# Transposing the normalized activations of three of four chunks by DMA in place of TensorE

## The chip, the core and the metric

The kernel runs on one core of a Trainium2 chip. The metric is the device time of one execution in microseconds (us), as the median of three runs; beside it stands one profiled execution, whose trace tells where each engine was busy. The engines are named as the profile names them: PE is TensorE (PEld its weight loads), DVE is VectorE, ACT is ScalarE, POOL is GpSimd, SP is SyncE, which here issues DMAs alone (SPq in the trace).

## The reference

The input `x` has 2048 rows of 512 bf16 values. Each row is normalized, and the result goes into two branches whose product is added to `x`:

```python
xn = _layernorm(x, axis=-1)
s = _A_ref(xn, A_wqkv, A_wo)                       # attention
g = _silu(_B_ref(xn, B_w_gate, B_w_up, B_w_down))  # gated MLP
return x + s * g
# A: q, k, v = xn @ wqkv; 32 heads of 16; each row attends to itself and
#    to the rows 2, 4, ..., 14 before it; softmax; output @ wo
# B: h = gelu(xn @ w_gate) * (xn @ w_up), 1792 wide; output h @ w_down
```

[...] the normalized rows (rows on partitions) have to be transposed (features on partitions) before the projections `wqkv`, `w_gate` and `w_up` can use them.

## The kernel before

The 2048 rows are 16 tiles of 128 rows, in 4 chunks of 512 (chunk j holds tiles 4j to 4j+3). The order of all instructions on each engine is written out by hand; engines meet through semaphores.

For each tile, `moments` (L169) takes mean and variance on VectorE and the reciprocal root on GpSimd, `normalize` (L179) writes the normalized tile `xn` (128x512) on VectorE, from a pool of four buffers, and `transpose` (L186) makes four 128x128 transposes on TensorE into one PSUM tile `tr`, which ScalarE copies (L194) to a quarter of `xnT`, the transposed chunk (128 x 4 x 512). `xnT` has two buffers; `xnT` of chunk 2 takes the place of chunk 0's.

For each chunk there are three stages, and the program's order is glu 0, qkv 1, down 0, glu 1, qkv 2, down 1, and so on, after a beginning that makes qkv 0:

- `qkv` j: 12 groups of four matmuls with `xnT` of chunk j: four each for q, k and v. ScalarE evicts each. The v part is stored through SyncE's queue to a DRAM tensor `vT` (L235), and `load_v` (L243) loads it back in another layout as `v_arr`, in four DMAs.
- `glu` j: 14 steps of `g_ps` and `u_ps` (four matmuls each), with Gelu and a copy on ScalarE (`ge`, `u`, three buffers each) and their product `h` on VectorE. PSUM has five buffers that all these results share.
- `down` j: for each tile 14 matmuls with `wd_sb` and four with `wo_sb`, then the product, the residual and the store of the output (L387).

The attention of chunk j is spread over these stages with the table `side`: `at(key, fn, ...)` (L395) places a function ahead of a step, and `run` calls it. The products q*k (`pk`), logits and exponentials come first; `av_product` (L311) makes `pv` from the exponentials and `v_arr` on VectorE, eight per chunk; `av_sums` sums four of them at a time on TensorE into `o_ps` (L325). For chunk 0, `pv` 0 and 1 stand at steps 12 and 13 of glu 0, `pv` 2 to 7 in qkv 1, and the first `o_ps` ahead of qkv 1's fourth group (step 3). For later chunks `pv` i stands at step 2+i of glu j and `o_ps` at step 7.

The same table places the layer norm: normalize of chunk 1 in qkv 0, its transposes at glu 0's first four steps; normalize of chunk 2 at steps 8 to 11 of glu 0, its transposes in qkv 1; normalize and transposes of chunk 3 in qkv 2.

SyncE issues nearly all DMAs, in program order: the loads of `x`, `wqkv`, `w_gate` and `w_up` at the start; the vT stores of chunk 0; its four `v_arr` loads; then `load_late_weights` (L102): `wd_sb`, 1792 KB, and four parts of `wo_sb`, 128 KB each. In the rest of the program come, for each chunk, four vT stores (in qkv), and in the down stage before it is used four `v_arr` loads, one ahead of each output store. An instruction of SyncE that waits holds up all that stand behind it. The completion semaphores of DMAs are eight, taken in turn, so that a DMA may have to wait until the one eight before it has landed.

Of the kernel before, what the change touches and what calls it, by code (L numbers as in the profile page):

```python
# [10 lines left out]
BF16 = mybir.dt.bfloat16  # L11
F32 = mybir.dt.float32

P = 128
# [7 lines left out]
TQ = 512  # L22
# [6 lines left out]
def kernel(  # L29
# [13 lines left out]
    nc = tc.nc  # L43
    B, S, D = A_x.shape
    DF = B_w_gate.shape[1]
    NT, NC, NF, NJ = S // P, D // P, DF // P, S // TQ
    TPQ = TQ // P
# [5 lines left out]
    def pool(name, bufs, **kw):  # L53
        return ctx.enter_context(tc.tile_pool(name=name, bufs=bufs, **kw))
# [9 lines left out]
    xtp = pool("xtp", 2)  # L64
# [38 lines left out]
    def load_late_weights():  # L103
        nc.sync.dma_start(out=wd_sb[:], in_=B_w_down.rearrange("(k p) n -> p k n", p=P))
        for g in range(NC):
            nc.sync.dma_start(
                out=wo_sb[:, g, :],
                in_=bass.AP(
                    tensor=A_wo.tensor, offset=g * 4 * D, ap=[[D, 4], [DH * D, H], [1, D]]
                ),  # L110
            )
# [7 lines left out]
        out=vT.rearrange("(k p) n -> p k n", p=P)[:, :, 0:PAD],  # L119
        in_=warm[:, 0 : NC * PAD].rearrange("p (k n) -> p k n", k=NC),  # L120
# [38 lines left out]
    xnT = {}  # L159
# [17 lines left out]
    xns = {}  # L177
# [22 lines left out]
    def warm_up(n, cols):  # L200

        ps = mm.tile([P, TQ], F32, name="warm_ps", tag="mm")
        for _ in range(n):
            nc.tensor.matmul(
                ps[:, 0:cols], lhsT=warm[:, 0:P], rhs=warm[:, 0:cols], start=True, stop=True
            )

    def project(ps, w, lo, j, i0=0, n=TQ):
        for dk in range(NC):
            nc.tensor.matmul(  # L210
                ps[:],
                lhsT=w[:, dk, lo : lo + P],
                rhs=xnT[j][:, dk, i0 : i0 + n],
                start=(dk == 0),
                stop=(dk == NC - 1),
            )
# [3 lines left out]
    def qkv(j, fo, i0=0, n=TQ):  # L220
        which, c = divmod(fo, NC)
        if fo == 0 and i0 == 0:
            st[j]["q"] = qp.tile([P, NC, TQ], BF16, name="q_sb")
        ps = mm.tile([P, n], F32, name="qkv_ps", tag="mm")
        project(ps, wqkv_sb, fo * P, j, i0, n)
        if which == 0:
            nc.scalar.activation(out=st[j]["q"][:, c, i0 : i0 + n], in_=ps[:], func=AF.Copy)  # L227
        elif which == 1:
            lo = PAD + j * TQ + i0
            nc.scalar.activation(out=k_sb[:, c, lo : lo + n], in_=ps[:], func=AF.Copy)  # L230
        else:
            vst = sm4.tile([P, TQ], BF16, name="vst")
            nc.scalar.activation(out=vst[:], in_=ps[:], func=AF.Copy)  # L233
            lo = PAD + j * TQ
            nc.sync.dma_start(out=vT[c * P : (c + 1) * P, lo : lo + TQ], in_=vst[:])  # L235

    def load_v(j, wls=range(WL)):

        if wls[0] == 0:
            st[j]["va"] = vap.tile([P, DH, VW], BF16, name="v_arr")  # L240
        va = st[j]["va"]
        for wl in wls:
            nc.sync.dma_start(  # L243
                out=va[H * wl : H * (wl + 1), :, :],
                in_=bass.AP(
                    tensor=vT.tensor,
                    offset=PAD + j * TQ - WL * DIL - DIL * wl,
                    ap=[[SV * DH, H], [SV, DH], [1, VW]],
                ),
            )  # L250
# [93 lines left out]
    def glu(j, fc):  # L344
        g_ps = mm.tile([P, TQ], F32, name="g_ps", tag="mm")
        project(g_ps, wg_sb, fc * P, j)
        u_ps = mm.tile([P, TQ], F32, name="u_ps", tag="mm")
        project(u_ps, wu_sb, fc * P, j)
        ge = sm.tile([P, TQ], BF16, name="ge")
        nc.scalar.activation(out=ge[:], in_=g_ps[:], func=AF.Gelu_apprx_tanh)  # L350
        u = sm.tile([P, TQ], BF16, name="u")
        nc.scalar.activation(out=u[:], in_=u_ps[:], func=AF.Copy)  # L352
        h = hp.tile([P, TQ], BF16, name="h")
        nc.vector.tensor_tensor(out=h[:], in0=ge[:], in1=u[:], op=ALU.mult)  # L354
        st[j][fc] = h
# [38 lines left out]
    def at(key, fn, *args):  # L394
        side.setdefault(key, []).append((fn, args))  # L395
# [5 lines left out]
    for i in range(TPQ):  # L401
        at(("qkv", 0, i), normalize, TPQ + i)
        at(("glu", 0, 7 + i), moments, 2 * TPQ + i)
        at(("glu", 0, i), transpose, TPQ + i)
        at(("glu", 0, 8 + i), normalize, 2 * TPQ + i)
        at(("qkv", 1, 1 + 3 * i), transpose, 2 * TPQ + i)
        at(("glu", 1, 10 + i), moments, 3 * TPQ + i)
        at(("qkv", 2, 2 * i), normalize, 3 * TPQ + i)
        at(("qkv", 2, 3 + 2 * i), transpose, 3 * TPQ + i)

    for w in range(W):
        at(("glu", 0, w), qk_product, 0, w)
# [50 lines left out]
    for i in range(NC):  # L463
        run("qkv", 0, i)
        run("qkv", 0, NC + i)
        qkv(0, 2 * NC + i)
    load_v(0)
    load_late_weights()
    for j in range(NJ):
        for fc in range(NF):  # L470
# [37 lines left out]
```

The softmax here doesn't subtract the row's maximum and nothing guards it: scores larger than these inputs give would overflow.

## Time and profile before

| | us |
|---|---|
| median of 3 runs (lowest, highest) | 234.64 (234.57, 234.67) |
| the profiled execution, whole | 234.66 |
| its span, from the first to the last instruction | 233.0 |
| PE busy (share of the span) | 227.3 (98%) |
| DVE busy | 146.4 (63%) |
| ACT busy | 135.6 (58%) |
| POOL busy | 23.4 (10%) |

The stages that matter here, with the span's start as zero:

| stage | from, to (us) | PE busy | DVE busy | ACT busy | share of the DMA engines |
|---|---|---|---|---|---|
| beginning and qkv 0 | 0 to 18.6 | 16.8 | 12.0 | 11.1 | 0.9 |
| glu 0 | 18.6 to 45.5 | 26.9 | 19.7 | 22.6 | 0.93 |
| qkv 1 | 45.5 to 59.3 | 13.8 | 11.7 | 9.6 | 0.18 |
| down 0 | 59.3 to 74.8 | 15.5 | 11.7 | 4.4 | 0.65 |
| glu 1 | 74.8 to 103.4 | 28.6 | 21.9 | 19.6 | 0.08 |
| qkv 2 | 103.4 to 114.7 | 11.3 | 5.1 | 9.1 | 0.05 |
| down 1 | 114.7 to 130.2 | 15.5 | 9.4 | 4.3 | 0.67 |

Matmuls are pipelined and their ends are modelled, so that the starts of successive matmuls say more than their lengths. In a line of the trace, "L210 PE MATMUL g_ps<-xnT,wg_sb ... x4" is: line of the kernel, engine, operation, what is written from what, sizes, how many. A timeline line begins with its start and length in us; "[0.44 <-POOL rstd L175]" at its end says that the engine was idle for 0.44 us before it, and what ended that wait.

### The profile page before, as it was taken

How to read it: one execution, taken by the hardware profiler on the slowest of the kernel's cores; microseconds unless marked ns; L12 is line 12 of the kernel's file. 1: busy time of each engine (PE TensorE's matmuls, PEld its weight loads, DVE VectorE, ACT ScalarE, POOL GpSimd, SP SyncE). 2: the span in 40 equal slices, each digit the busy share in tenths (PEclk: the TensorE clock that was granted, in tenths of full speed). 3: DMA queues.
4: the chain of work that ended last, by engine and by line, in shares of the span. 5: the costliest groups of instructions: out<-in, count | busy, mean ns of one | idle time of the engine just before them, and what ended most of it. 6: DMA issues, size and time to landing. Idle time of an engine off the chain costs nothing.

```text
span 233.0 us, 3523 instructions
## 1 busy us (share of the span) xinstructions
PE 227.3 (98%) x1345; PEld 106.0 (46%) x1345; DVE 146.4 (63%) x232; ACT 135.6 (58%) x222; POOL 23.4 (10%) x64
## 2 busy tenths in 40 slices
PE   7999999999999999999999999999999999999993
PEld 2775444444444444445444444444444444444441
DVE  4593996996795198981669139951349429864132
ACT  2779869777513865758821396657641387576211
POOL 3248923100000000130000000000000000000000
PEclk9999999999999999999999999999999999999999
DMA  5999499821288200000267600000047810000001
GB/s 151 361 374 367 109 212 210 273 76 48 72 184 199 49 0 0 3 0 0 83 140 174 154 1 3 0 0 3 23 126 169 197 34 0 0 3 1 23 23 45
DMA packets 21937, 22.66 MB, mean 97 GB/s; under 512 B 1568, under 2 KB 21920, under 8 KB 21920
## 3 DMA queue, kind: packets, MB, share of 16 engines
q1 hardware_dynamic: 21776, 22.37, 36.1%
q8 instruction: 10, 0.16, 0.3%
q10 hardware_dynamic: 144, 0.07, 0.1%
q14 instruction: 7, 0.06, 0.1%
HBM read 18.22 MB, written 4.21 MB: 96 GB/s over the span
## 4 chain that ended last, share of the span: by engine, by line
PE 95%; DVE 2%; DMA 1%; ACT 1%; issue 0%
PE g_ps L210 21%; PE u_ps L210 21%; PE y_ps L360 21%; PE qkv_ps L210 18%; PE s_ps L377 6%; PE o_ps L325 3%; PE L_ps L265 3%; PE tr L190 2%; DMA x_sb<-in_A_x_dram 1%; DVE stats L170 1%; PE den_ps L285 0%; PE sp_ps L300 0%; DVE m L385 0%; ACT xnT L194 0%; ACT sl L368 0%; DVE o_t L386 0%
## 5 line engine op out<-in xcount | busy, mean ns | idle before, releaser
L210 PE MATMUL g_ps<-xnT,wg_sb 128*128 128x512 bf16 x224 | 57.6, 379 | 0.0
L210 PE MATMUL u_ps<-xnT,wu_sb 128*128 128x512 bf16 x224 | 57.5, 379 | 0.0
L360 PE MATMUL y_ps<-wd_sb,h 128*128 128x512 bf16 x224 | 51.0, 379 | 0.0
L255 DVE TENSOR_TENSOR pk<-q_sb,k_sb 128x2048 bf16<-128x2048 bf16 x32 | 37.8, 1220 | 12.2 <-ACT k_sb L230 12.2
L354 DVE TENSOR_TENSOR h<-ge,u 128x512 bf16<-128x512 bf16 x56 | 23.7, 423 | 34.2 <-ACT u L352 34.2
L210 PE MATMUL qkv_ps<-xnT,wqkv_sb 128*128 128x512 bf16 (+1 forms) x224 | 44.2, 349 | 0.5 <-ACT xnT L194 0.5
L350 ACT ACTIVATE ge<-g_ps 128x512 bf16<-128x512 f32 x56 | 33.6, 601 | 14.4 <-PE g_ps L210 12.9
L352 ACT ACTIVATE u<-u_ps 128x512 bf16<-128x512 f32 x56 | 33.6, 600 | 13.9 <-PE u_ps L210 13.9
L311 DVE TENSOR_TENSOR pv<-E,v_arr 128x2048 bf16<-128x2048 bf16 x32 | 38.6, 1216 | 0.0
L368 ACT ACTIVATE sl<-y_ps 128x512 bf16<-128x512 f32 x16 | 9.6, 597 | 43.9 <-PE y_ps L360 43.9
L210 PEld LDWEIGHTS <-wu_sb 128*128 128x128 bf16 x224 | 21.9, 98 | 26.6 <-issue 0.3
L360 PEld LDWEIGHTS <-h 128*128 128x128 bf16 x224 | 22.0, 98 | 26.4
L210 PEld LDWEIGHTS <-wg_sb 128*128 128x128 bf16 x224 | 20.8, 98 | 26.7 <-issue 4.2
L210 PEld LDWEIGHTS <-wqkv_sb 128*128 128x128 bf16 x224 | 21.3, 98 | 18.3 <-issue 0.7
L385 DVE TENSOR_TENSOR m<-s_ps,sl 128x512 bf16<-128x512 f32 (+1 forms) x17 | 11.2, 658 | 26.8 <-PE s_ps L377 24.4
L175 POOL TENSOR_TENSOR rstd<-rstd,mhalf 128x1 f32<-128x1 f32 x16 | 10.4, 652 | 79.1 <-DVE rstd L172 79.1
L377 PE MATMUL s_ps<-wo_sb,oT 128*128 128x512 bf16 (+1 forms) x68 | 16.4, 366 | 0.0
L170 DVE BATCH_NORM_STATS2 stats<-x_sb 128x6 f32<-128x512 bf16 x16 | 11.0, 686 | 4.1 <-DMA x_sb<-in_A_x_dram 4.1
L227 ACT ACTIVATE q_sb<-qkv_ps 128x512 bf16<-128x512 f32 (+1 forms) x20 | 10.2, 512 | 4.7 <-PE qkv_ps L210 4.4
L233 ACT ACTIVATE vst<-qkv_ps 128x512 bf16<-128x512 f32 x16 | 9.6, 597 | 5.0 <-PE qkv_ps L210 5.0
L194 ACT ACTIVATE xnT<-tr 128x512 bf16<-128x512 bf16 x16 | 9.5, 597 | 4.2 <-PE tr L190 4.2
L230 ACT ACTIVATE k_sb<-qkv_ps 128x512 bf16<-128x512 f32 (+1 forms) x20 | 10.2, 512 | 2.1 <-PE qkv_ps L210 1.9
(42 smaller groups left out, 121.5 us busy)
## 6 DMA issues: line engine op xcount, KB each, us to landing
v_arr<-vT SPq DMA_DIRECT2D x16, 520.0 KB, 5.1
vT<-vst SPq DMA_DIRECT2D x16, 128.0 KB, 1.7
out_dram<-o_t SPq DMA_DIRECT2D x15, 128.0 KB, 2.6
wg_sb<-in_B_w_gate_dram SPq DMA_DIRECT2D x2, 896.0 KB
wu_sb<-in_B_w_up_dram SPq DMA_DIRECT2D x2, 896.0 KB, 13.2
wd_sb<-in_B_w_down_dram SPq DMA_DIRECT2D x1, 1792.0 KB, 16.9
wqkv_sb<-in_A_wqkv_dram SPq DMA_DIRECT2D x3, 512.0 KB, 5.7
x_sb<-in_A_x_dram SPq DMA_DIRECT2D x3, 512.0 KB, 10.0
```

The lines of the kernel that those rows point to most:

```text
L170: nc.vector.bn_stats(out=stats[:, t, :], in_=x_sb[:, t, :])
L175: nc.gpsimd.tensor_tensor(out=rstd[:, t, :], in0=rstd[:, t, :], in1=mhalf[:], op=ALU.pow)
L210: nc.tensor.matmul(ps[:], lhsT=w[:, dk, lo : lo + P], rhs=xnT[j][:, dk, i0 : i0 + n], start=(dk == 0), stop=(dk == NC - 1),)
L227: nc.scalar.activation(out=st[j]["q"][:, c, i0 : i0 + n], in_=ps[:], func=AF.Copy)
L255: nc.vector.tensor_tensor(out=pk[:], in0=st[j]["q"][:], in1=k_sb[:, :, off : off + TQ], op=ALU.mult)
L311: nc.vector.tensor_tensor(out=pv[:], in0=st[j]["E"][:, wh, :].unsqueeze(1).to_broadcast([P, 4, TQ]), in1=st[j]["va"][:, 4 * g : 4 * g + 4, ...
L350: nc.scalar.activation(out=ge[:], in_=g_ps[:], func=AF.Gelu_apprx_tanh)
L352: nc.scalar.activation(out=u[:], in_=u_ps[:], func=AF.Copy)
L354: nc.vector.tensor_tensor(out=h[:], in0=ge[:], in1=u[:], op=ALU.mult)
L360: nc.tensor.matmul(y[:], lhsT=st[j][fc][:, tt * P : (tt + 1) * P], rhs=wd_sb[:, fc, :], start=(fc == 0), stop=(fc == NF - 1),)
L377: nc.tensor.matmul(s[:], lhsT=st[j]["oT"][:, g, tt * P : (tt + 1) * P], rhs=wo_sb[:, g, cols], start=(g == 0), stop=(g == NC - 1),)
L385: nc.vector.tensor_tensor(out=m[:], in0=s[:], in1=sl[:, cols], op=ALU.mult)
```

## The change

The tiles of chunk 0 are transposed by TensorE as before. Those of chunks 1 to 3 are transposed by DMA, straight from `xn` to `xnT`, both in SBUF: four DMAs of 128x128 for each tile, all issued by SyncE. There is no PSUM tile and no copy on ScalarE for them.

```diff
+    def transpose_by_dma(ts):
+        for t in ts:
+            j, i = divmod(t, TPQ)
+            if i == 0:
+                xnT[j] = xtp.tile([P, NC, TQ], BF16, name="xnT")
+            for c in range(NC):
+                nc.sync.dma_start(
+                    out=xnT[j][:, c, i * P : (i + 1) * P],
+                    in_=xns[t][:, c * P : (c + 1) * P],
+                    transpose=True,
+                )
...
     for i in range(TPQ):
         at(("qkv", 0, i), normalize, TPQ + i)
         at(("glu", 0, 7 + i), moments, 2 * TPQ + i)
-        at(("glu", 0, i), transpose, TPQ + i)
         at(("glu", 0, 8 + i), normalize, 2 * TPQ + i)
-        at(("qkv", 1, 1 + 3 * i), transpose, 2 * TPQ + i)
         at(("glu", 1, 10 + i), moments, 3 * TPQ + i)
         at(("qkv", 2, 2 * i), normalize, 3 * TPQ + i)
-        at(("qkv", 2, 3 + 2 * i), transpose, 3 * TPQ + i)
+        at(("down", 1, i), transpose_by_dma, [3 * TPQ + i])
+    at(("qkv", 1, 0), transpose_by_dma, range(2 * TPQ, 3 * TPQ))
...
     load_v(0)
+    transpose_by_dma(range(TPQ, 2 * TPQ))
     load_late_weights()
```

So 48 transposing DMAs are added to SyncE's queue: 16 for chunk 1 between the `v_arr` loads of chunk 0 and `wd_sb`; 16 for chunk 2 behind `wo_sb` and ahead of chunk 1's vT stores; and for chunk 3 four ahead of each of the four `v_arr` loads in down 1. They are numbered T1 to T48 in that order below. Normalizing is where it was; since a normalized tile's buffer is free only when its four transposes have read it, normalize of tile 8+i now waits for the transposes of tile 4+i, as it waited for TensorE's before.

## Prediction

> **What bounds the kernel now.** I read the page's chain first, then the groups, then each stage's timeline. The chain that ended last is TensorE's:
>
> ```profile
> PE 95%; DVE 2%; DMA 1%; ACT 1%; issue 0%
> ```
>
> So TensorE work that is removed is worth its full time, if nothing makes TensorE wait instead. What one transposed tile costs there is read from TensorE's timeline across the end of glu 0 and the start of qkv 1 (start, length):
>
> ```profile
> 44.52 1.03 PE L210 MATMUL u_ps<-xnT,wu_sb 128*128 128x512 bf16 x4
> 45.39 1.03 PE L210 MATMUL qkv_ps<-xnT,wqkv_sb 128*128 128x512 bf16 x4
> 46.25 0.39 PE L190 MATMUL tr<-ident,xn 128*128 128x128 bf16 x4
> 46.48 1.89 PE L210 MATMUL qkv_ps<-xnT,wqkv_sb 128*128 128x512 bf16 x8
> 48.30 0.30 PE L285 MATMUL den_ps<-E,hsum 128*32 128x128 bf16 x8
> 48.42 1.04 PE L325 MATMUL o_ps<-pv,hsum 128*32 128x512 bf16 x16
> ```
>
> Ends are modelled and overlap; starts tell: four transposes take 46.48 - 46.25 = 0.23 us, four 128x512 matmuls 0.86 us. There are no gaps: qkv 1 begins as glu 0 ends, at 45.4, and o_ps follows at 48.42.
>
> Now the queue that gets the work, SyncE's, in the same stretch:
>
> ```profile
> 27.31 2.69 SPq L243 DMA_DIRECT2D v_arr<-vT  x4
> 30.05 0.66 SPq L104 DMA_DIRECT2D wd_sb<-in_B_w_down_dram  x1
> 30.75 14.89 SPq L106 DMA_DIRECT2D wo_sb<-in_A_wo_dram  x4
> ```
>
> The longest time to landing of any v_arr load is
>
> ```profile
> DMA to landing us min/median/max: 5.0/5.1/11.4
> ```
>
> and belongs to the last of these four: issued at 29.34, it lands at 40.7. Four back to back thus take 27.3 to 40.7, 13.4 us. The 16 transposes of chunk 1 are put between the first and the second line of that view.
>
> VectorE in the same stretch:
>
> ```profile
> 42.96 0.41 DVE L181 TENSOR_SCALAR xn<-x_sb,mv,rstd 128x512 bf16<-128x512 bf16 x1 [0.44 <-POOL rstd L175]
> 43.29 0.42 DVE L354 TENSOR_TENSOR h<-ge,u 128x512 bf16<-128x512 bf16 x1
> 43.63 1.22 DVE L311 TENSOR_TENSOR pv<-E,v_arr 128x2048 bf16<-128x2048 bf16 x1
> 44.76 0.42 DVE L354 TENSOR_TENSOR h<-ge,u 128x512 bf16<-128x512 bf16 x1
> 45.10 1.22 DVE L311 TENSOR_TENSOR pv<-E,v_arr 128x2048 bf16<-128x2048 bf16 x1
> 46.28 0.43 DVE L354 TENSOR_TENSOR h<-ge,u 128x512 bf16<-128x512 bf16 x1
> 46.62 3.49 DVE L311 TENSOR_TENSOR pv<-E,v_arr 128x2048 bf16<-128x2048 bf16 x3
> ```
>
> From the last normalize of chunk 2 (42.96) there is no slack: three h and four pv follow back to back, and the fourth pv ends at 48.97, just as o_ps, which reads it, runs. VectorE busy is only 63% over the span, but here it is on the edge.
>
> [...] wd_sb, issued 0.7 us after the last v_arr load, lands 16.9 us later, after v_arr's 40.7. [...] The nine 128x512 warm-up matmuls agree, 4.02 us in all, 0.45 each against 0.22 later.
>
> **The unknown price, c,** is the time between successive 128x128 transposes on SyncE's queue; the trace has none. Nearest rows: plain issues on that queue take 0.32 (vT) to 0.67 us. [...] I take 1.31[...]. Landing: 1.4 us after the issue's end, as the vT stores (1.7 less 0.32).
>
> **Part by part.**
>
> *Removed.* Twelve tiles' transposes: 12 x 0.22 = 2.6 us of TensorE, all on the chain; 12 evictions of 0.60 us on ScalarE, 7.1 us, beside TensorE and so worth nothing.
>
> *Added, chunk 1.* T1 to T16 stand behind four v_arr loads. The order on SyncE shows that each DMA waits for the landing of the one eight before it. T1 to T4 may be issued from 30.05, but [...]they land after 40.7. T5 to T8 wait for the four v_arr landings, so T8 is issued at 40.7 or later whatever c is. T9 waits for T1 (about 42). Then T16's issue ends at 42.0 + 8 x 1.31 = 52.5 and it lands at 53.9. In the work before, these transposes were done by glu 0's fourth step.
>
> Two things wait. qkv 1 needs all 16 (45.4, or 44.5 without four groups of PE transposes). And the four xn buffers make VectorE's normalize of tile 8+i wait for the four transposes that read tile 4+i; behind it in VectorE's order stand h and pv. TensorE can run on to the end of glu 0 (three ge/u and five PSUM buffers), but after T16 lands VectorE still has normalize, three h and four pv, 6.0 us as in the view above, while qkv 1's first three groups cover 2.6. So o_ps is late by what the last normalize is late: 53.9 - 42.96 = 10.9 us. This includes the five transposed groups that are gone before o_ps; the other seven give back 7 x 0.22 = 1.5 us.
>
> *Moved, wd_sb and wo_sb.* Behind T16: wd issued by 53.2, then 6.3 us for its data (40.7 to 47.0 before), 59.5; wo about 5.9 us more (46.6 to 52.4 in the page's GB/s row), 65.4. First use is down 0, at 59.1 + 10: hidden; it would cost the difference if c were small and chunk 1 on time, and then it is issued earlier too.
>
> *Added, chunk 2.* T17 to T32 follow wo; the last waits on it end at 65.4, eight more transposes give 66.7 + 8 x 1.31 = 77.2. Queued behind them are chunk 1's vT stores (before: 56.1): issued by 78.5, landed 79.9, then v_arr 13.4 us, 93.3. VectorE's first pv of chunk 1, before at 81.56, is due at 92.5, and its o_ps has 1.3 us of slack: hidden, but with nothing over.
>
> *Added, chunk 3.* In down 1 each v_arr load and out store gets four transposes ahead of it. SyncE before:
>
> ```profile
> 117.30 0.55 SPq L243 DMA_DIRECT2D v_arr<-vT  x1
> ...
> 128.07 0.55 SPq L243 DMA_DIRECT2D v_arr<-vT  x1
> ```
>
> After, on that clock: vT issued by 115.7; plus 16 x 1.31 = 21.0, plus three v_arr and three out issues 2.7 gives 139.4 for the last v_arr, landing 5.1 later, 144.5. The pv that needs it starts at 138.32 before, with 0.6 us of slack to o_ps: 144.5 - 138.9 = 5.6 us of stall.
>
> *Clock.* The 9 us stall before qkv 1 is repaid inside the 6.0 us that TensorE waits for pv anyway; the stall in glu 2 leaves the array cold: 1.7 to 2 us.
>
> *Sum.* 10.9 + 0 + 5.6 - 1.5 + 2 = 17.0. The profiled execution took 234.66 (span 233.0 and 1.7 around it), the median is 234.64: about 252 us.
>
> **Rivals.**
>
> *Cheap issue, c near 0.53.* T16 issued by 41.5 + 8 x 0.53 = 45.8, landed 47.2; 4.2 us late at o_ps, chunks 2 and 3 hidden: 234.64 + 4.2 - 1.5 = 237.4. For it: plain issues here cost 0.3 to 0.67. [...] Chance 0.25, times 236 to 242.
>
> *Issue and data in series, c near 1.84.* Chunk 1: 30.05 + 29.4 + 1.4 = 60.9, 17.9 late. Chunk 2: T32 by 95.4, v_arr landed 111.5 against 100.8: 10.7. Chunk 3: 29.4 in place of 21.0 gives 14.0. Sum 42.6 - 1.5 and some 3.5 of cold clock: 279. [...]against: eight may be in flight. Chance 0.20, with dearer transposes above.
>
> *Hidden altogether, not slower.* The place is the queue behind v_arr in glu 0. If all 16 land by 44.9 the delay of 2.0 us is repaid by the 1.5 us left over and VectorE's edge, and earlier ones tend to 232.0. T8 cannot start before 40.7, so nine issues and 1.4 us of landing must fit in 4.2 us: c at most 0.31, just under the cheapest issue in the trace (0.32). Chance 0.05.
>
> *Main case*, c from 0.95 to 1.6: 242 (T16 landed by 51) to 267 (chunk 2's v_arr late too). Chance 0.50.
>
> **How the numbers follow.** The predicted time is the main case at 1.31. The range goes down to the cheap case and up to the serial one, 237 to 280; about 9 in 100 lie on each side. A change within 0.2% (0.5 us) can't be told from none. Faster 0.04 is nearly all of the hidden case; same 0.02 is its edge and that of the cheap case; slower 0.94.
>
> **What would show it.** Transposes on SyncE between 30 and 53 with the first landings after 40; VectorE's normalize in glu 0 ended by a DMA; TensorE idle before qkv 1, then before its o_ps; wd_sb issued after 50; pv of chunk 2 ended by v_arr landing near 144 plus the shift. Wrong: a c outside 0.53 to 1.84; transposes that don't queue behind v_arr; a delay in a stage not named here, such as wd_sb late for down 0.

## The result

The kernel takes 261.6 us after the change (median of 6 runs, 260.7 to 262.4) against 234.6 before (6 runs): a ratio of 1.115, 95% interval 1.113 to 1.117. The forecast was 252, with a range of 237 to 280.

The profiled execution's span grew from 233.0 to 259.9 us, by 26.9. The chain that ended last is no longer TensorE's alone:

```profile
PE 63%; DMA 12%; DVE 12%; SPq 10%; issue 1%; ACT 1%; POOL 0%; DVEq 0%; ACTq 0%
```

SyncE's queue (SPq), absent from it before, holds a tenth of the span, and DMAs and VectorE another quarter. The transposing DMAs as a group, with the length of the issuing instruction on SyncE in ns (min/median/max), and their time to landing:

```profile
L214 SPq DMA_TRANSPOSE xnT<-xn x48: 1098/1230/2166, 30.2 to 157.2; - x48
...
DMA to landing us min/median/max: 2.3/2.6/12.9
```

So c, the unknown of the prediction, is 1.23 us and the 0.04 us to the next: 1.27. The best landing, 2.3 us after the issue's start, is 1.1 us after its end. SyncE's timeline (start, length):

```profile
27.47 2.66 SPq L255 DMA_DIRECT2D v_arr<-vT  x4
30.18 23.41 SPq L214 DMA_TRANSPOSE xnT<-xn  x16
53.62 0.58 SPq L104 DMA_DIRECT2D wd_sb<-in_B_w_down_dram  x1
54.26 5.66 SPq L106 DMA_DIRECT2D wo_sb<-in_A_wo_dram  x4
60.04 21.87 SPq L214 DMA_TRANSPOSE xnT<-xn  x16
82.01 2.34 SPq L247 DMA_DIRECT2D vT<-vst  x4
```

From 30.2 to 84.4 this queue is never free: it issues, or it waits. First come 16 transposes, then the late weights, then 16 more transposes, and only then the vT stores of chunk 1. Before they began here:

```profile
56.07 4.21 SPq L235 DMA_DIRECT2D vT<-vst  x4
```

The first 16 took 23.4 us, more than 16 times 1.27: the eighth was issued at 41.2, after the queue had waited 1.8 us for the last `v_arr` load to land, as the prediction had it. SyncE's waits show it (us in total, times, longest):

```profile
SPq L214 <- DMA v_arr<-vT: 1.9, 2, 1.8
```

VectorE shows the two kinds of wait that follow, with what ended each in brackets:

```profile
33.97 0.42 DVE L366 TENSOR_TENSOR h<-ge,u 128x512 bf16<-128x512 bf16 x1
44.86 0.41 DVE L181 TENSOR_SCALAR xn<-x_sb,mv,rstd 128x512 bf16<-128x512 bf16 x1 [10.47 <-DMA xnT<-xn]
...
54.81 0.41 DVE L181 TENSOR_SCALAR xn<-x_sb,mv,rstd 128x512 bf16<-128x512 bf16 x1 [3.18 <-DMA xnT<-xn]
...
100.16 1.23 DVE L323 TENSOR_TENSOR pv<-E,v_arr 128x2048 bf16<-128x2048 bf16 x1 [7.42 <-DMA v_arr<-vT]
...
164.12 1.22 DVE L323 TENSOR_TENSOR pv<-E,v_arr 128x2048 bf16<-128x2048 bf16 x1 [8.51 <-DMA v_arr<-vT]
```

In glu 0 normalize waits for the transposes that free its buffer. In glu 1 and glu 2 the first pv waits for `v_arr`, a load that the change didn't touch but that stands behind transposes. Before, the first pv of chunk 1 had no wait:

```profile
81.56 1.22 DVE L311 TENSOR_TENSOR pv<-E,v_arr 128x2048 bf16<-128x2048 bf16 x1
```

TensorE around chunk 0's first o_ps:

```profile
42.90 1.03 PE L222 MATMUL g_ps<-xnT,wg_sb 128*128 128x512 bf16 x4
47.35 1.02 PE L222 MATMUL u_ps<-xnT,wu_sb 128*128 128x512 bf16 x4 [3.42 <-ACT ge L362]
...
54.73 3.96 PE L222 MATMUL qkv_ps<-xnT,wqkv_sb 128*128 128x512 bf16 x9 [0.63 <-DMA xnT<-xn]
...
61.15 1.90 PE L222 MATMUL qkv_ps<-xnT,wqkv_sb 128*128 128x512 bf16 x8
```

The wait reached TensorE inside glu 0 (the last u_ps at 47.35), then qkv 1 ran matmul by matmul as each transpose of the last tile landed, and from 54.7 at half rate (nine matmuls in 3.9 us, 0.43 each against 0.22; the granted clock was 0.51 from 54.7 to 58.6).

Where the 26.9 us arose is read from the start of the same group on TensorE in both traces:

| TensorE reaches | before | after | later by |
|---|---|---|---|
| qkv 1 after chunk 0's first o_ps | 49.4 | 61.2 | 11.8 |
| down 0 | 59.1 | 70.2 | 11.1 |
| glu 1 after chunk 1's first o_ps | 89.9 | 106.4 | 16.5 |
| glu 1 after chunk 1's second o_ps | 99.8 | 118.0 | 18.1 |
| down 1 | 114.6 | 131.8 | 17.2 |
| glu 2 after chunk 2's first o_ps | 145.5 | 170.4 | 24.9 |
| glu 2 after chunk 2's second o_ps | 155.4 | 182.4 | 26.9 |

Chunk 1's transposes cost 11.8 us, chunk 2's 5.4 and 1.6 of cold clock after the stall, chunk 3's 7.7 and 2.0; the transposes gone from qkv 1 and qkv 2 gave back 0.7 and 0.9. "Cold clock" stands for the stretches at half rate that followed waits in these runs, such as the one from 54.7, at a granted clock of 0.51. In glu 1 it shows in the starts after o_ps:

```profile
106.40 1.89 PE L222 MATMUL g_ps<-xnT,wg_sb 128*128 128x512 bf16 x4
...
109.74 1.03 PE L222 MATMUL g_ps<-xnT,wg_sb 128*128 128x512 bf16 x4
```

From the first start to the second, eight matmuls take 3.3 us, where the same eight took 1.7 before. The granted clock was 0.50 from 106.4 to 109.7, and 1.00 from there to 114.

### The profile page after: what moved, and what is told of

It is laid out like the page before. It is cut to its first block, busy times and chain, and to the rows that moved or that the text cites. A ratio compares the mean times of both kernels' runs of the same rounds, so it can differ in the third digit from the quotient of the medians.

```text
span 259.9 us, 3484 instructions
## 1 busy us (share of the span) xinstructions
PE 235.0 (90%) x1297; PEld 104.7 (40%) x1297; DVE 146.2 (56%) x232; ACT 129.4 (50%) x210; POOL 26.3 (10%) x64
## 4 chain that ended last, share of the span: by engine, by line
PE 63%; DMA 12%; DVE 12%; SPq 10%; issue 1%; ACT 1%; POOL 0%; DVEq 0%; ACTq 0%
PE qkv_ps L222 15%; PE y_ps L372 15%; PE g_ps L222 12%; PE u_ps L222 12%; SPq L214 8%; DMA v_arr<-vT 6%; DVE pv L323 5%; DMA xnT<-xn 5%; PE s_ps L389 4%; PE o_ps L337 2%; DVE h L366 1%; SPq L399 1%; DVE pk L267 1%; DVE stats L170 1%; SPq L255 1%
## 5 line engine op out<-in xcount | busy, mean ns | idle before, releaser
L222 PE MATMUL u_ps<-xnT,wu_sb 128*128 128x512 bf16 x224 | 59.2, 388 | 3.4 <-ACT ge L362 3.4
L222 PE MATMUL g_ps<-xnT,wg_sb 128*128 128x512 bf16 x224 | 59.7, 390 | 0.0
L222 PE MATMUL qkv_ps<-xnT,wqkv_sb 128*128 128x512 bf16 (+1 forms) x224 | 46.0, 362 | 5.0 <-DMA xnT<-xn 4.5
L222 PEld LDWEIGHTS <-wg_sb 128*128 128x128 bf16 x224 | 21.4, 100 | 29.1 <-issue 7.0
L222 PEld LDWEIGHTS <-wqkv_sb 128*128 128x128 bf16 x224 | 21.9, 99 | 27.0 <-DMA xnT<-xn 6.5
L337 PE MATMUL o_ps<-pv,hsum 128*32 128x512 bf16 x128 | 11.4, 430 | 11.2 <-DVE pv L323 11.2
L181 DVE TENSOR_SCALAR xn<-x_sb,mv,rstd 128x512 bf16<-128x512 bf16 x16 | 6.1, 413 | 16.1 <-DMA xnT<-xn 14.7
```

The source lines that it names most:

```text
L222: nc.tensor.matmul(ps[:], lhsT=w[:, dk, lo : lo + P], rhs=xnT[j][:, dk, i0 : i0 + n], start=(dk == 0), stop=(dk == NC - 1),)
L337: nc.tensor.matmul(o[H * i : H * (i + 1), g, :], lhsT=hsum[:], rhs=st[j]["pv"][2 * gg + g, wh][:, i, :], start=(wh == 0), stop=(wh == WH - 1),
```

## The experiments

**Theories.** A: what costs is SyncE's issue, 1.27 us for each transposing instruction one after another, and what stands behind it in that queue is late. B: the transposes' data are slow, or disturb other transfers. C: the delay comes from the four xn buffers, through which VectorE waits for the transposes. All ratios are to the kernel before, run beside, with their 95% intervals.

**One chunk at a time.** Each of these keeps the change for one chunk and restores TensorE's transposes for the other two; for chunk 1:

```diff
-        at(("down", 1, i), transpose_by_dma, [3 * TPQ + i])
-    at(("qkv", 1, 0), transpose_by_dma, range(2 * TPQ, 3 * TPQ))
+        at(("qkv", 1, 1 + 3 * i), transpose, 2 * TPQ + i)
+        at(("qkv", 2, 3 + 2 * i), transpose, 3 * TPQ + i)
```

> Chunk 1 alone is transposed by DMA (16 transposing DMAs between chunk 0's v_arr loads and wd_sb); chunks 2 and 3 by TensorE as before. Theory A (SyncE issues a 128x128 transpose in 1.24 us, one after the other, and what stands behind them is late): the delay at chunk 0's first o_ps stays what the full change has, +11.8 us, and nothing else is late: 246.4 us. Theory B[...]: the same delay here. Theory C (the wait of normalize for xn buffers makes the delay): the same here. The run tells whether chunk 1's share is independent of the other two.

Measured: 246.58 us, 1.051 (1.0495 to 1.0526). Chunk 1's 12.0 us stand by themselves. All three theories had forecast this, so the run says only that.

> Chunk 2 alone by DMA. Theory A: SyncE is free from 45.7 to 56 us, so T17 to T32 run from 45.7 to about 67, chunk 1's vT stores and v_arr loads come some 8 us later than before but mostly still in time for the first pv of chunk 1 at 81.6: between 233.7 (hidden, 0.9 us of TensorE saved) and 236. In the full change the same 16 cost 7.0 us less 0.9, because they start at 60 behind chunk 1's. Theory B: the 16 transposes cost about what they cost in the full change, 240 us.

Measured: 236.37 us (235.8 to 238.5), 1.0105 (1.0055 to 1.0155): slightly above A's upper end, and far from B's 240. The same 16 transposes now start at 45.6. The last `v_arr` load of chunk 1 lands at 84.6 and its first pv starts at 84.73, where it would be due near 80.9 (81.56 less what TensorE is ahead), so "mostly in time" was too hopeful by some 2 us.

> Chunk 3 alone by DMA, four transposes ahead of each v_arr load in down 1. Theory A: the last v_arr load of chunk 2 is issued some 13 us later than before, o_ps in glu 2 stalls by 7.7 us, cold clock adds 2.0, 0.9 of TensorE is saved: 243.4 us. Theory B: the same stall. If the parts were independent, the three alone would add up to the full change's +27.0; theory A expects them to add up to about 21 to 22.

Measured: 242.89 us, 1.0354 (1.0334 to 1.0374). The three add up to 12.0 + 1.8 + 8.3 = 22.0 us, where the full change costs 27.0: 5 us come from the parts together.

**Where the 5 us are.** The full change with chunk 2's transposes alone moved, to the start of glu 1:

```diff
-    at(("qkv", 1, 0), transpose_by_dma, range(2 * TPQ, 3 * TPQ))
+    at(("glu", 1, 0), transpose_by_dma, range(2 * TPQ, 3 * TPQ))
```

> The full change with chunk 2's 16 transposes alone moved, from the start of qkv 1 to the start of glu 1 (behind down 0's stores). Theory A: chunk 1's vT stores and v_arr loads no longer stand behind them, so the 7.0 us that glu 1 lost (5.4 of stall, 1.6 of cold clock) are gone and the rest stays: 254.6 us. If chunk 2's delay were not from the queue but from chunk 1's lateness handed on, nothing changes: 261 us.

Measured: 254.78 us, 1.0843 (1.0812 to 1.0874). SyncE's timeline of this kernel, and VectorE's first pv of chunk 1:

```profile
72.58 0.63 SPq L255 DMA_DIRECT2D v_arr<-vT  x1
...
87.83 17.54 SPq L214 DMA_TRANSPOSE xnT<-xn  x13
```

```profile
92.41 1.22 DVE L323 TENSOR_TENSOR pv<-E,v_arr 128x2048 bf16<-128x2048 bf16 x1
```

The first `v_arr` load goes out at 72.6 in place of 86.0 and pv has no wait. (13 is what lies in the window shown.) So glu 1's loss needs these 16 in that place; chunk 1's lateness on TensorE alone doesn't make it. The place alone doesn't either: in `only2` the same place costs 2.6 us (1.75 measured and 0.85 of work that left TensorE), where in the full change it costs 6.9. The rest comes from where the 16 start, at 45.6 alone and at 60.0 behind chunk 1's transposes and the late weights, and that is most of the 5 us.

**What the price is of.** Same bytes, other numbers of instructions. In halves (64x128 each):

```diff
-                nc.sync.dma_start(
-                    out=xnT[j][:, c, i * P : (i + 1) * P],
-                    in_=xns[t][:, c * P : (c + 1) * P],
+                for r in (0, 64):
+                    nc.sync.dma_start(
+                        out=xnT[j][:, c, i * P + r : i * P + r + 64],
+                        in_=xns[t][r : r + 64, c * P : (c + 1) * P],
```

> The full change, with two transposing DMAs of 64x128 in place of each of 128x128: 96 in all, same bytes. Theory A with a price per instruction: SyncE needs 2.5 us for what took 1.24, some 20 us more for each chunk: 310 us or more. Theory A with a price per piece: 261 us. Theory B (data bound): 261 us.

Measured: 321.06 us, 1.368 (1.362 to 1.375). And whole tiles (128x512, the output as 128x4x128):

```diff
-            for c in range(NC):
-                nc.sync.dma_start(
-                    out=xnT[j][:, c, i * P : (i + 1) * P],
-                    in_=xns[t][:, c * P : (c + 1) * P],
-                    transpose=True,
-                )
+            nc.sync.dma_start(
+                out=xnT[j][:, :, i * P : (i + 1) * P], in_=xns[t][:], transpose=True
+            )
```

> The full change, with one transposing DMA for a whole tile (128x512 to 128x4x128) in place of four of 128x128: 12 in all, same bytes. Theory A with a price per instruction: four issues of 1.24 us for chunk 1 end by 36, their data land right behind v_arr at about 42.5, normalize of chunk 2 is not late, chunks 2 and 3 are hidden: 232 to 233 us. Theory A with a price per piece of data inside the instruction (four times the data, four times the issue): nothing changes, 261 us.

Measured: 242.26 us, 1.030 (1.025 to 1.035). The transposing DMAs of the halves, then of the whole tiles:

```profile
L215 SPq DMA_TRANSPOSE xnT<-xn x96: 1088/1226/1955, 30.4 to 217.6; - x96
```

```profile
L213 SPq DMA_TRANSPOSE xnT<-xn x12: 1197/1328/3189, 30.3 to 135.8; - x12
```

64x128, 128x128 and 128x512 take 1.23, 1.23 and 1.33 us to issue in the median: the price is per instruction, from 16 to 128 KB. (Five of the twelve of `whole`, which stand right behind `v_arr` or `wo_sb`, took longer, 1.8 to 3.2 us each.) With B, the same bytes should have taken the same time. But `whole` did not come to 232: its VectorE shows why.

```profile
42.99 0.41 DVE L181 TENSOR_SCALAR xn<-x_sb,mv,rstd 128x512 bf16<-128x512 bf16 x1 [8.71 <-DMA xnT<-xn]
...
45.19 0.41 DVE L181 TENSOR_SCALAR xn<-x_sb,mv,rstd 128x512 bf16<-128x512 bf16 x1 [0.45 <-POOL rstd L175]
...
49.58 0.41 DVE L181 TENSOR_SCALAR xn<-x_sb,mv,rstd 128x512 bf16<-128x512 bf16 x1 [0.44 <-POOL rstd L175]
```

The first normalize of chunk 2 waits until 42.99 for the first transpose to land, behind `v_arr`. Before the next one stand VectorE's moments of the next tile and a power on GpSimd, 2.2 us for each round; the last normalize comes at 49.58 against 42.96 before, 6.6 us late, with all transposes long landed (45.0). TensorE is 6.8 us late behind o_ps (56.15 against 49.39) and 8.6 us at down 0 (67.70 against 59.14), for after the wait it ran cold:

```profile
56.15 3.59 PE L219 MATMUL qkv_ps<-xnT,wqkv_sb 128*128 128x512 bf16 x8
```

Eight such matmuls have a length of 1.89 us in the trace of before; the granted clock of `whole` was 0.87 from 43.8 to 70.3, and 1.00 in the stretches on both sides of it. Later stages lose nothing more, and 0.9 comes back in qkv 2.

**The same with plain copies.**

```diff
                 nc.sync.dma_start(
                     out=xnT[j][:, c, i * P : (i + 1) * P],
                     in_=xns[t][:, c * P : (c + 1) * P],
-                    transpose=True,
                 )
```

> The full change with plain 128x128 copies in place of the transposing DMAs: same number, same bytes, same queue and waits; the transposition itself is left out, so that the matmuls work on untransposed data. Theory A: a plain issue costs 0.3 to 0.6 us, T16 lands by 48, chunks 2 and 3 are hidden: 237 to 239 us. Theory B: the plain copy of 256-byte rows is no cheaper in data than the transpose, 255 us or more. Theory C: the waits are all still there; above 245 us.

Measured: 241.36 us, 1.028 (1.022 to 1.033), above A's figure, and below B's 255 and C's 245. The issue:

```profile
L214 SPq DMA_DIRECT2D xnT<-xn x48: 465/599/1351, 30.1 to 137.7; - x48
```

Half the price of a transposing one, 20 us less in the whole. What A's figure lacked is again the chain of normalize and the cold clock after it (a mean granted clock of 0.986 over the execution, against 0.999 before): the first normalize waits until 42.12, the last runs at 48.70, 5.7 us late, and TensorE is 5.9 us late behind o_ps and 7.6 at down 0.

**Eight xn buffers**, first with four DMAs per tile, then with one:

```diff
+    xp = pool("xp", 8)
-        xn = xns[t] = sm4.tile([P, D], BF16, name="xn")
+        xn = xns[t] = xp.tile([P, D], BF16, name="xn")
```

> The full change with eight buffers for xn in place of four, so that normalize of chunk 2 waits for no transpose. Theory A: qkv 1 still waits for T16 at 54.7, but VectorE's h and pv are no longer behind normalize, so o_ps comes 2.6 us after qkv 1's start instead of 6: about 3 us less, 258.5 us. Theory C (the buffer wait is what makes chunk 1's delay): about 250 us.

Measured: 262.09 us, 1.116 (1.111 to 1.121): no gain, where A had expected 258.5 and C 250. VectorE is now done with pv long before TensorE needs it, but TensorE isn't earlier by much. VectorE, then TensorE, of this kernel:

```profile
45.56 3.49 DVE L324 TENSOR_TENSOR pv<-E,v_arr 128x2048 bf16<-128x2048 bf16 x3
```

```profile
54.71 3.59 PE L223 MATMUL qkv_ps<-xnT,wqkv_sb 128*128 128x512 bf16 x8 [0.63 <-DMA xnT<-xn]
...
60.04 1.25 PE L223 MATMUL qkv_ps<-xnT,wqkv_sb 128*128 128x512 bf16 x5
```

qkv 1 still waits for the last landing at 54.7 and then runs cold, eight matmuls in 3.6 us (granted clock 0.81 from 43.8 to 70.3); o_ps is over at 60.04 instead of 61.15. That 1.1 us is lost again in glu 1: its pv waits for `v_arr` until 100.83, since SyncE's schedule has not moved. With dear issue C falls: the wait for buffers is real, but two others stand behind it, qkv 1's for the last transpose and glu 1's for `v_arr`.

> The full change in its own places, with one transposing DMA per whole tile and eight buffers for xn. With cheap issue chunk 1 still was 6.8 us late, and its trace has normalize of tile 8 waiting until 43.0 for the first transpose, whose data lie behind v_arr, and then four rounds of normalize, moments and rstd of 2.2 us each. Theory C in this setting: without the buffer wait only qkv 1's wait for the last landing at about 45.0 remains, 233 to 234 us. Theory A without C (the landing alone is what counts): 241 us, as with four buffers.

Measured: 233.66 us (233.2 to 236.3), 0.9958 (0.9930 to 0.9987). With cheap issue C holds: the same eight buffers are worth 8.6 us against `whole` (by the medians).

**Places where SyncE was idle.** Chunk 1 by TensorE, the other two moved:

```diff
-        at(("down", 1, i), transpose_by_dma, [3 * TPQ + i])
-    at(("qkv", 1, 0), transpose_by_dma, range(2 * TPQ, 3 * TPQ))
+        at(("glu", 0, i), transpose, TPQ + i)
+    at(("glu", 1, 0), transpose_by_dma, range(2 * TPQ, 3 * TPQ))
+    at(("glu", 2, 0), transpose_by_dma, range(3 * TPQ, 4 * TPQ))
...
-    transpose_by_dma(range(TPQ, 2 * TPQ))
```

> Chunk 1 by TensorE; chunks 2 and 3 by DMA, but their transposes stand on SyncE where the trace of before shows it idle: chunk 2's at the start of glu 1 (after the last output store of down 0), chunk 3's at the start of glu 2. Same number of transposes per chunk, same data. Theory A: 16 x 1.25 = 20 us of issue fit in both gaps (76.5 to 103.5 and 132 to 159), nothing waits, and TensorE saves 8 x 0.22 = 1.76 us: 232.9 us. Theory B (slow data disturbs other work wherever it stands, or the transposes last longer than their issue): 234.6 or more.

Measured: 233.12 us (232.9 to 233.2), 0.9935 (0.9920 to 0.9950). 32 transposes of 1.27 us cost nothing where nobody waits for SyncE, and TensorE is shorter by what left it. B, with 234.6 or more, falls here too.

Last, one DMA per tile (as in `whole`), chunks 2 and 3 placed as above, and chunk 1 ahead of `load_v(0)`:

```diff
-    load_v(0)
     transpose_by_dma(range(TPQ, 2 * TPQ))
+    load_v(0)
```

> All three chunks by DMA, one transposing DMA for each whole tile (12 in all, 1.24 us of SyncE each), placed where SyncE was idle: chunk 1's four ahead of chunk 0's v_arr loads (the trace of before has SyncE waiting from 21.7 to 27.3 for the vT stores to land), chunk 2's at the start of glu 1, chunk 3's at the start of glu 2. Theory A: nothing waits for them and TensorE saves all 12 groups of 0.22 us: 232.0 us. Theory B (data of transposes disturbs v_arr or the stores): 233.5 or more. Theory C (normalize still waits for xn buffers): no wait either, since chunk 1's transposes land by 28 and the first normalize of chunk 2 runs at 35.

Measured: 233.11 us (232.5 to 233.9), 0.9929 (0.9902 to 0.9956); its profiled execution took 232.46. SyncE:

```profile
16.94 4.76 SPq L244 DMA_DIRECT2D vT<-vst  x4
21.79 6.35 SPq L213 DMA_TRANSPOSE xnT<-xn  x4
28.32 2.65 SPq L252 DMA_DIRECT2D v_arr<-vT  x4
```

The four transposes sit where SyncE waited for the vT stores to land; `v_arr` goes out 1.0 us later than before. In the profiled execution, the fastest of the six, TensorE reaches its last stage 2.2 us earlier than before, so no wait cost anything there. The median stands between A's 232.0 and B's 233.5 and decides for neither; why the other executions took up to 1.4 us longer is not shown. This version, `late23` and `whole8` are all faster than the kernel before, by under 1%, and so than the changed one; the intervals don't separate them from each other.

## Why the prediction was right, and where it was off

**Removed work** was right: TensorE's groups cost 0.22 to 0.23 us; those in qkv 1 and qkv 2 gave back 1.6 us against 1.5 forecast.

**The sum** was 17.0 us, and 26.9 were measured in the profiled execution. Of the 9.9 us that were missing, chunk 2 made 7.0, chunk 3 made 2.1 and chunk 1 made 0.9; the removed work gave 0.1 more than forecast. That the time still lies inside the range is owed to the range's width: the main case had chunk 2 hidden, and named its `v_arr` as late only at its upper end.

**Issue price c**: 1.31 was taken, 1.27 measured. The value was an assumption, as were the 0.53 and the 1.84 of the rivals; the trace of before has no transposing DMA and shows none of the three. That 1.31 came close is in part luck. In the runs it is the issue that holds SyncE: it takes 1.23 us with half the data and with the whole, four times the data take 0.1 us more, and 128x128 transposes that don't stand behind other transfers land 1.1 us after it. Cheap issue at 0.53 didn't occur: the shortest transposing issue in any run was 1.09 us. Nor did 1.84 as a price: the medians lie between 1.23 and 1.33.

**Chunk 1** was right, in number and path: T1 landed at 43.1, 12.9 us after its issue began and behind the last `v_arr` load's 41.2 (forecast about 42), T16 landed at 54.7 (forecast 53.9), the last normalize came at 54.81, and o_ps was late by 11.8 us (10.9). One statement in that part was wrong: TensorE did not run on to the end of glu 0 unharmed; its last u_ps waited for VectorE. It cost nothing, as qkv 1 had to wait longer anyway. The cold clock before o_ps (0.51 from 54.7) was free, as forecast, since VectorE came still later. The margin was small: with eight buffers, where only TensorE's own path is left, o_ps was over just 1.1 us earlier. In `whole` and `plain` TensorE waits ahead of o_ps and is cold after it, and there the clock was not free.

**Chunk 2** failed: "hidden, but with nothing over" was 5.4 us of stall and 1.6 of cold clock. The step that failed is its issue time, T32 by 77.2 against 81.9: I let T17 to T24 go out while wo_sb landed, but SyncE was held by the issue of wo_sb until 59.9, and 16 transposes from there took 21.9. The vT stores then took 2.3 us to issue in place of 1.3, and the loads, interleaved with output stores that were waiting too, 14.1 in place of 13.4. The serial rival's own T32, 95.4, comes out if all 16 follow wo_sb's issue (66.0 + 29.4); counted so, the main case would have had T32 at 80.1 and a stall. A sum with nothing over should have been forecast as one. That these 16, in that place, are needed for it is shown by `late2`, 6.9 us faster.

**Chunk 3** was right in kind: 7.7 us of stall against 5.6. The last `v_arr` load went out at 158.48, where 139.4 + 17.2 of shift makes 156.6; the three output stores ahead of it took 0.62, 1.69 and 0.56 us to issue, where 0.34 each was taken. Cold clock 2.0 (granted clock 0.50 from 170.4 to 174.5) against 1.7 to 2, which was an estimate of mine.

**Rivals.** The cheap case's 237.4 and the hidden case's threshold of 0.31 us were both wrong by one step: I carried normalize's lateness from the last landing alone. From the first landing behind `v_arr` VectorE's four normalizes follow in rounds of 2.2 us, a floor that no c removes. At half the price (`plain`) and at a quarter of the instructions (`whole`) that floor remained, 5.7 and 6.6 us, and the cold clock after it, which the cheap case put at nothing, added a net 1.7 and 1.8 by down 0. In the places of the change and with four buffers, neither cheaper DMA won; other places or more buffers did.

## What to carry to other kernels

Count the DMA instructions that a change adds to a queue, not their bytes: here a transposing DMA held SyncE for 1.2 to 1.3 us (median) from 16 to 128 KB, so one for 128x512 did the work of four, and what stood behind them in program order was late: chunk 1's vT stores, behind 32 of them, began at 82.0 in place of 56.1. Put such work where the trace shows the queue idle, and check which loads of other stages stand behind it. A pool whose buffers are now freed later makes a second wait, here 10.5 us ahead of chunk 2's first normalize. Eight buffers alone gave nothing, whole tiles alone left the kernel 3% slower than before, and both together came to 233.7 us: so try both.

## What was not expected of the hardware

A transposing DMA's issue took the same 1.2 to 1.3 us in the median for 16, 32 and 128 KB, twice a plain DMA of the same 128x128 shape (0.60). After the stalls in glu 1 and glu 2 TensorE stayed at half rate for some 3 and 4 us once it had work again: the granted clock was 0.50 from 106.4 to 109.7 and from 170.4 to 174.5, which added 1.6 and 2.0 us after the waits.
